# Cosine attention with a routed feed-forward: GpSimd's products held behind the transposes, gate rows spread over slots, square sums before the tail scores, and the last two batches' routed layers interleaved

## The chip, the cores and the metric

One core of a Trainium2 chip runs the whole program. The metric is device time in microseconds from the start of the program to its end. Engines: PE (matrix multiply; PEld is its weight load), DVE (vector), ACT (scalar), POOL (GpSimd), SP (issues DMAs). Each works through its own instructions in order and waits on semaphores for the others.

## The reference

```python
q_n = q / (norm(q) + 1e-6);  k_n = k / (norm(k) + 1e-6)      # (8, 12, 448, 64)
attn = softmax(q_n @ k_n.T / 0.1)
x = (attn @ v).transpose(0, 2, 1, 3).reshape(8, 448, 768)
scores = einsum('bsd,d->bs', x, w_gate)
for b in range(8):                                           # capacity 128
    top = the 128 rows of batch b with the largest scores
    xe = x[b, top]
    out[b, top] = x[b, top] + sigmoid(scores[b, top]) * (relu(xe @ w1) @ w2)   # w1 (768, 1024)
# all other rows of out are x
```

## The kernel before

**Attention.** The 96 heads are handled as 48 pairs, 6 pairs to a batch. Pair i has a *slot* i of the main loop (lines 591 to 641); the schedule is manual, so the order in which the code calls its helpers is the order of the instructions on every engine. The work of a slot is software-pipelined over four pairs:

- `square(p)` (L196, ACT) squares q and k of a pair about five slots ahead; `sum_pe` (L203, PE) and `sum_dve` (L209) add the squares up; `norm_a` (L217, L218, ACT) and `norm_b` (L223, L226, DVE) make the reciprocal norms for a group of up to three pairs.
- `scale(i+2)` (L236) multiplies q and k by the reciprocal norms into a buffer `qkn`, with two POOL instructions, and `values(i+2)` (L243, POOL) casts v. There are four `qkn` buffers (`NB`, L141).
- `transposes(i+1)` (L252 full tiles, L257 tails) turns them on PE into `qkT_ps`, and `qkT_copy` (L271, DVE) takes them to SBUF.
- `scores(i, c)` (L282; L287 for the tail c = 3) and `exps(i, c)` (L295; L298 for the tail) make the exponentials. They use a ring of two PSUM tiles `sc`, of two banks each; the sums of the squares go into the second bank of the tail's tile.
- `pv_tails(i-1)` and `pv(i-1)` (L309, L321) make the product with v, and `pv_evac` (L334, L335, DVE) divides by the row sums into `x_b`.

**Routed layer (MoE).** It runs batch by batch, woven into later slots. `at(slot, where, ...)` hangs a step on one of a slot's places (P, D1, A, D2, P2, C, B0, B), and the main loop calls the places in a fixed order. D1 and D2 stand before and after `pv_evac`, A between them, B at the slot's end. Its steps: `gate` (L357, DVE, one instruction for each of four row tiles j, two inputs in SBUF: `x_b` and `wg_b`), `rank_prep` (L366 to L375, POOL), `rank_rep` (L384, L387, PE), four `rank_count` (L396, DVE), four picks (L405, POOL) that make the one-hot `sel`, `select` (L416, PE, and L419 to L423, DVE), `gather` in two parts (L455, PE), `ffn1` in two halves (L469), `ffn2` in two halves (L482), and a scatter with add into the output (L488, an indirect DMA from POOL). All PSUM results of this layer share one bank (`bank`, L378). `store_x` (L344 to L349) writes x to the output from SP and a bf16 copy `xh` through POOL's queue, in two parts.

The last batch has its gates in three parts, over slots 46 to 48, and all its other steps stand after the loop (lines 644 to 656), each after the one before. Batch 6's `ffn1` second half and `ffn2` are in slot 48.

**Loads.** `load` (L98 to L114) issues eleven DMAs for a group of up to three pairs, from SP save for the keys of group 0, which ACT issues. Four raw buffers are used in turn. `load_wg` (L184) is the gate's weight, spread over 128 partitions, issued in slot 3; the weights w1 and w2 (L181) are loaded through POOL's queue in slots 3 and 6. `warm(n)` (L563) issues n idle matmuls of zeros.

Of the kernel before, what the change touches and what calls it, by code (L numbers as in the profile page):

```python
# [17 lines left out]
def kernel(  # L18
# [12 lines left out]
    nc = tc.nc  # L31
# [92 lines left out]
    load(1, 1, nc.sync)  # L124
    load(0, 2, nc.sync)
    load(1, 2, nc.sync)
    for which in range(3):
        load(2, which, nc.sync)

    iden_b = const.tile([P, P], BF16)  # L130
# [11 lines left out]
    kn_bufs = [const.tile([P, 2, NS, P], BF16, name=f"qkn{n}") for n in range(NB)]  # L142
# [18 lines left out]
    tie = const.tile([P, NS, S], BF16)  # L161
    iden_f = const.tile([P, P], FP32)
    ones_f = const.tile([P, P], FP32)
    nc.vector.memset(tie, 0.0)
    nc.vector.memset(ones_f, 1.0)
    wg_b = const.tile([P, D], FP32)
# [3 lines left out]
    def consts_a():  # L170
        nc.gpsimd.tensor_copy(iden_f, iden_b)

    def consts_tie(j):
        nc.gpsimd.affine_select(
            out=tie[:, j, :], in_=tie[:, j, :], compare_op=ALU.is_ge,
            fill=-(2.0 ** -126), base=-j * P, pattern=[[1, S]],
            channel_multiplier=-1)
# [35 lines left out]
    def norm_a(n):  # L213
        gn = NORMS[n][1]
        rs = prep.tile([P, 3, 2, NB7], FP32, name="rs", bufs=3)
        rs_tiles[n] = rs
        nc.scalar.activation(rs[:, :gn], ss_tiles[n][:, :gn], AF.Ln)  # L217
        nc.scalar.activation(rs[:, :gn], rs[:, :gn], AF.Exp, scale=0.5)  # L218

    def norm_b(n):  # L220
        gn = NORMS[n][1]
        r = rs_tiles[n][:, :gn].rearrange("p g a b -> p (g a b)")
        nc.vector.scalar_tensor_tensor(  # L223
            out=r, in0=r, scalar=1e-6, in1=zeros[:, :gn * 2 * NB7],
            op0=ALU.add, op1=ALU.add)
        nc.vector.reciprocal(r, r)  # L226

    def scale(p, engines=None):
        gi, g = place[p]
        n, m = nplace[p]  # L230
        qk = raw[gi % NRAW][0]
        rs = rs_tiles[n]
        kn = kn_bufs[p % NB]
        for eng, b0, nb, o in zip(engines or (nc.gpsimd, nc.gpsimd),
                                  (0, NS), (NS, NC), (0, Dh)):
            eng.tensor_mul(  # L236
                kn[:, :, :nb, o:o + Dh], qk[:, :, g, b0:b0 + nb],
                rs[:, m, :, b0:b0 + nb].rearrange("p a (b o) -> p a b o", o=1)
                .to_broadcast([P, 2, nb, Dh]))
# [7 lines left out]
    def transposes(p, part):  # L247
        kn = kn_bufs[p % NB]
# [26 lines left out]
    def scores(i, c):  # L275
        qkT = qkT_tiles[i]
        sc = ps_sc.tile([P, 2, 512], FP32, name="sc")
# [64 lines left out]
    def store_x(b):  # L342
        x_b = x_tiles[b]
        nc.sync.dma_start(out=out[b, :SM].rearrange("(m c) d -> m c d", c=NC),  # L344
                          in_=x_b[:, :NC])
        nc.sync.dma_start(out=out[b, SM:S], in_=x_b[:T, NC])
        xh = xp.tile([P, NS, D], BF16, name="xh")
        nc.gpsimd.dma_start(out=xh[:, :NC], in_=x_b[:, :NC])
        nc.gpsimd.dma_start(out=xh[:T, NC], in_=x_b[:T, NC])  # L349
        xh_tiles[b] = xh  # L350
# [27 lines left out]
    def bank():  # L378
        return ps_m.tile([P, 512], FP32, name="m_ps")
# [21 lines left out]
    def pick(b):  # L401
        sel = moe.tile([P, NS, CAP], BF16, name="sel")
        for j in range(NS):
            n = rows(j)
            nc.gpsimd.tensor_scalar(  # L405
                out=sel[:n, j], in0=iota_r[:n], scalar1=ranks[b % 2][:n, j:j + 1],
                scalar2=None, op0=ALU.is_equal)
        st[b]["sel"] = sel

    def select(b):  # L410
        sel, sg = st[b]["sel"], st[b]["sg"]
        pk = bank()
        for o, w, src in ((0, 2, tokc), (2, 3, sg)):
# [4 lines left out]
        pks = moe.tile([P, 2], FP32, name="pks")  # L418
        nc.vector.tensor_copy(pks, pk[:, 0:2])  # L419
        gr = moe.tile([P, 1], FP32, name="gr")  # L420
        nc.vector.tensor_reduce(gr, pk[:, 2:5], axis=AX.X, op=ALU.add)
        idx = moe.tile([P, 1], I32, name="idx")
        nc.vector.scalar_tensor_tensor(  # L423
            out=idx, in0=pks[:, 0:1], scalar=float(b * S), in1=pks[:, 1:2],
            op0=ALU.add, op1=ALU.add)
        st[b].update(idx=idx, gr=gr)

    def select_b(b):
        gr = st[b]["gr"]
        nc.scalar.activation(gr, gr, AF.Exp, scale=-1.0)  # L430
        nc.vector.scalar_tensor_tensor(out=gr, in0=gr, scalar=1.0, in1=zeros[:, :1],
                                       op0=ALU.add, op1=ALU.add)
        nc.vector.reciprocal(gr, gr)
# [12 lines left out]
    def gather(b, part, eng="D"):  # L446
# [3 lines left out]
        t0, t1 = ((0, 4), (4, KD))[part]  # L450
        ps = bank()
# [9 lines left out]
    def ffn1(b, part, eng="D"):  # L461
# [3 lines left out]
        ps = bank()  # L465
# [9 lines left out]
    def ffn2(b, n, eng="D"):  # L475
        hT = st[b]["hT"]
        if n == 0:
            st[b]["oe"] = moe.tile([P, D], FP32, name="oe")
        oe = st[b]["oe"]
        ps = bank()  # L480
        for t in range(KF):
# [3 lines left out]
        evac(eng, oe[:, n * ND:(n + 1) * ND], ps[:, :ND], AF.Copy,  # L485
             st[b]["gr"])
        if n == 1:
            nc.gpsimd.indirect_dma_start(  # L488
                out=out_flat[:, :],
                out_offset=bass.IndirectOffsetOnAxis(ap=st[b]["idx"][:CAP, 0:1],  # L490
                                                     axis=0),
                in_=oe[:CAP], in_offset=None, compute_op=ALU.add)
# [11 lines left out]
    for b in range(B - 2):  # L504
        s = HP * (b + 1)
        for j, (d, w) in enumerate(((1, "D1"), (1, "D2"), (2, "D1"), (2, "D2"))):
            at(s + d, w, gate, b, j)
        at(s + 3, "P", rank_prep, b)
        at(s + 3, "B", rank_rep, b)
        for j in range(NS):  # L510
            at(s + 4, "D1" if j < 2 else "D2", rank_count, b, j)
        at(s + 4, "P2", pick, b)
        at(s + 5, "A", select, b)
        at(s + 5, "C", select_b, b)
        at(s + 5, "B", gather, b, 0)
        at(s + 6, "A", gather, b, 1)
        at(s + 6, "B", ffn1, b, 0)
        late = b < B - 3
        at(s + 7, "B" if late else "A", ffn1, b, 1)
        at(s + 7 + late, "B", ffn2, b, 0)  # L520
        at(s + 8 + late, "A", ffn2, b, 1)
    b, bb = B - 2, B - 1
    s = HP * bb
    for j, (d, w) in enumerate(((0, "D2"), (1, "D1"), (1, "D1"), (1, "D2"))):
        at(s + d, w, gate, b, j)
    at(s + 2, "P", rank_prep, b)
    at(s + 2, "B0", rank_rep, b)
    for j in range(NS):
        at(s + 3, "D1" if j < 2 else "D2", rank_count, b, j)
    at(s + 3, "P2", pick, b)  # L530
    at(s + 4, "A", select, b)
    at(s + 4, "C", select_b, b)
    at(s + 4, "B", gather, b, 0)
    at(s + 5, "A", gather, b, 1)
    at(s + 5, "B", ffn1, b, 0)
    at(s + 6, "A", ffn1, b, 1, "A")
    at(s + 6, "A", ffn2, b, 0, "A")
    at(s + 6, "A", ffn2, b, 1, "A")
    ga = const.tile([P, NS], FP32)
    gb = const.tile([P, NS], FP32)  # L540
    for j in range(NS):
        at(N - 2, "D2", gate, bb, j, 0, 4 * P, None, ga)
        at(N - 1, "D2", gate, bb, j, 4 * P, 5 * P, ga, gb)
        at(N, "D2", gate, bb, j, 5 * P, D, gb)
    for b in range(B):
        at(HP * (b + 1), "D2", store_x, b)
    for j in range(NS):
        at(j, "P", consts_tie, j)
    at(0, "P", consts_a)
    at(3, "D1", load_wg)  # L550
    at(3, "P", load_w, w1_sb, moe_w1, kn_bufs[1][:, 1, 0, 0:1])
    at(6, "P", load_w, w2_sb, moe_w2, kn_bufs[0][:, 1, 0, 0:1])
# [12 lines left out]

    warm(30)
    for n in (0, 1):
        g0, gn = NORMS[n]
        sc = ps_sc.tile([P, 2, 512], FP32, name="sc")
        dst = [sc[:, 1, m * SW:(m + 1) * SW] for m in range(gn)]  # L570
        for m in range(gn):
            square(g0 + m)
        for m in range(gn):
            sum_pe(g0 + m, dst[m])
            sum_dve(g0 + m, dst[m])
        norm_a(n)
        norm_b(n)
        if n == 0:
            warm(50)
            scale(0, (nc.gpsimd, nc.vector))  # L580
            values(0)
# [3 lines left out]
        else:  # L585
            scale(1)
            values(1)
# [3 lines left out]
    for i in range(N + 1):  # L591
# [5 lines left out]
        run(i, "P")  # L597
# [6 lines left out]
        if live:  # L604
            exps(i, 0)
            exps(i, 1)
            for p in SQ.get(i, []):
                square(p)
# [5 lines left out]
        run(i, "P2")  # L614
        if i + 2 < N:
            scale(i + 2)
            values(i + 2)
# [4 lines left out]
        if live:  # L622
            scores(i, 3)
        if nxt:
            transposes(i + 1, 1)
            qkT_copy(i + 1)
        if live:
            exps(i, 2)
            sc = sc_tiles[i, 3]
            exps(i, 3)  # L630
            for m, p in enumerate(SQ.get(i, [])):
                dst = sc[:, 1, m * SW:(m + 1) * SW]
                sum_pe(p, dst)
                sum_dve(p, dst)
                n, g = nplace[p]
                if g == NORMS[n][1] - 1:
                    norm_a(n)
                    norm_b(n)
        run(i, "C")
        run(i, "B0")  # L640
        run(i, "B")
    assert not work, work

    rank_prep(bb)
    rank_rep(bb)
    for j in range(NS):
        rank_count(bb, j)
    pick(bb)
    select(bb)
    gather(bb, 0, "A")  # L650
    select_b(bb)
    gather(bb, 1, "D")
    ffn1(bb, 0, "A")
    ffn1(bb, 1, "D")
    ffn2(bb, 0, "A")
    ffn2(bb, 1, "D")
# [35 lines left out]
```

## Time and profile before

| | |
|---|---|
| median of 2 runs | 369.77 us (368.88 to 370.67) |
| the profiled execution | 371.18 us, of which 369.4 us are the span of the profile |
| PE busy | 281.0 us, 76% of the span |
| DVE busy | 206.6 us, 56% |
| ACT busy | 198.5 us, 54% |
| POOL busy | 178.8 us, 48% |
| mean granted PE clock | 0.892 |
| moved by DMA | 56.80 MB, 154 GB/s over the span |
| loop from slot 8 to the start of slot 48 | 69.96 to 326.58 us |
| from the last PV evacuation (329.2 us) to the end | 40.2 us |

In a line of the profile, `L203 PE MATMUL sc<-sq,iden_b` is the line of the kernel, the engine, the operation, and what is written from what. In the page's table of groups follow the shape, the number of instructions, their busy time and mean, and then how long the engine stood idle just before them and on whom it waited. A line of a timeline has the start, the duration and, in brackets, the idle time before. A busy share is a mean over the span; a stage's limit is read from its own timeline.

### The profile page before, as it was taken

To read this page: it belongs to the slowest core of one execution; us is meant where nothing else is said; L and a number is where in the kernel's file an instruction comes from. 1 tells how busy PE (TensorE), PEld (TensorE's weight loads), DVE (VectorE), ACT (ScalarE), POOL (GpSimd) and SP (SyncE) were. 2 spreads that over 40 slices of the span, in tenths; PEclk is the share of its full clock that TensorE was granted. 3 is DMA by queue.
4 is the path that set the end of the run, shared out by engine and by line. 5 is a ranking of instruction groups with operands and counts; after the bars stand their busy time and mean duration, and the time that the engine had idled before them with its cause. 6 is when DMAs were issued, how large, how long until landed. Compare 5 with 4: busy or idle time off the path is not lost.

```text
span 369.4 us, 8858 instructions
## 1 busy us (share of the span) xinstructions
PE 281.0 (76%) x3617; PEld 198.5 (54%) x3617; DVE 206.6 (56%) x476; ACT 198.5 (54%) x291; POOL 178.8 (48%) x267
## 2 busy tenths in 40 slices
PE   5729878587968887878798886979597878983570
PEld 5626555365754665556656565656465655662350
DVE  1213432657594669667865678566857786650300
ACT  2436787467655664767456674667557636320010
POOL 1347355347542947284825683566358528005201
PEclk9955898679998999999969999999999999577587
DMA  5799999999992859775963879596211533005503
GB/s 154 185 243 244 224 245 248 223 285 237 284 222 69 174 176 215 156 144 158 263 155 49 220 206 182 101 227 192 39 17 30 170 57 44 2 0 89 178 0 43
DMA packets 52744, 56.80 MB, mean 154 GB/s; under 512 B 9824, under 2 KB 48224, under 8 KB 51680
## 3 DMA queue, kind: packets, MB, share of 16 engines
q1 hardware_dynamic: 47616, 44.22, 45.0%
q0 software_dynamic: 4768, 11.80, 20.4%
q8 instruction: 28, 0.46, 0.5%
q10 hardware_dynamic: 320, 0.23, 0.2%
q14 instruction: 12, 0.10, 0.1%
HBM read 39.71 MB, written 14.16 MB: 146 GB/s over the span
## 4 chain that ended last, share of the span: by engine, by line
PE 34%; ACT 19%; DVE 14%; DMA 13%; issue 12%; SPq 3%; POOL 2%; POOLq 1%; DVEq 0%; ACTq 0%
ACT expS L295 12%; DMA qk_raw<-in_q_dram 7%; PE o_ps L321 7%; PE m_ps L482 6%; PE m_ps L455 5%; PE sc L282 5%; PE sc L203 4%; DVE junk L357 4%; ACT sq L196 3%; DMA wg_b<-in_moe_w_gate_dram 3%; DVE junk L396 3%; SPq L114 3%; ACT expS L298 3%; PE m_ps L469 3%; DVE qkT L271 2%
## 5 line engine op out<-in xcount | busy, mean ns | idle before, releaser
L295 ACT ACTIVATE expS<-sc 128x896 bf16<-128x896 f32 x144 | 126.7, 915 | 92.8 <-PE sc L282 92.0
L236 POOL TENSOR_TENSOR qkn<-qk_raw,rs 128x384 bf16<-128x384 f32 (+1 forms) x95 | 91.8, 1032 | 26.0 <-DVE rs L226 12.8
L321 PE MATMUL o_ps<-vo,expS 128*128 128x65 bf16 (+1 forms) x1152 | 64.5, 202 | 0.0
L203 PE MATMUL sc<-sq,iden_b 128*128 128x112 bf16 x384 | 29.5, 226 | 45.8 <-ACT expS L298 41.4
L282 PE MATMUL sc<-qkT 64*128 64x448 bf16 x288 | 50.5, 383 | 15.2 <-DVE qkT L271 13.2
L321 PEld LDWEIGHTS <-expS 128*128 128x128 bf16 (+1 forms) x1152 | 51.2, 104 | 10.0
L203 PEld LDWEIGHTS <-iden_b 128*128 128x128 bf16 x384 | 25.7, 105 | 51.8 <-issue 51.1
L357 DVE CUSTOM_DVE_ANT_0 junk<-x_b,wg_b 128x768 bf16<-128x768 f32 (+3 forms) x32 | 48.3, 1510 | 4.6 <-DMA wg_b<-in_moe_w_gate_dram 4.5
L196 ACT ACTIVATE sq<-qk_raw 128x896 bf16<-128x896 f32 x48 | 45.3, 951 | 6.7 <-DMA v_raw<-in_v_dram 4.3
L488 POOL DMA_INDIRECT out_dram<-oe,idx x8 | 13.6, 1701 | 64.8 <-DVE oe L442 44.5
L271 DVE COPY qkT<-qkT_ps 128x960 bf16<-128x960 bf16 x48 | 31.3, 652 | 14.8 <-PE qkT_ps L252 14.8
L334 DVE RECIPROCAL rden<-o_ps 128x8 f32<-128x8 f32 x48 | 9.9, 206 | 45.7 <-PE o_ps L321 45.6
L243 POOL CAST vo<-v_raw 128x448 bf16<-128x448 f32 x48 | 35.1, 731 | 0.5 <-DMA v_raw<-in_v_dram 0.5
L335 DVE TENSOR_TENSOR x_b<-o_ps,rden 128x512 f32<-128x512 f32 x48 | 33.2, 691 | 1.7
L209 DVE TENSOR_REDUCE ss<-sc 128x14 f32<-128x112 f32 x48 | 13.0, 272 | 31.8 <-PE sc L203 31.3
L366 POOL TENSOR_TENSOR diag<-iden_f,gate 128x512 f32<-128x512 f32 x8 | 8.9, 1117 | 41.4 <-DVE gate L357 41.4
L482 PE MATMUL m_ps<-w_sb,hT 128*128 128x384 bf16 x128 | 26.1, 351 | 3.5 <-DVE hT L438 1.5
L469 PE MATMUL m_ps<-xeT,w_sb 128*128 128x128 bf16 x384 | 26.5, 231 | 2.9 <-DVE hT L438 1.7
L282 PEld LDWEIGHTS <-qkT 64*128 64x128 bf16 x288 | 12.6, 95 | 29.7 <-DVE qkT L271 16.6
L405 POOL TENSOR_SCALAR sel<-iota_r,rank 128x128 bf16<-128x128 bf16 (+1 forms) x32 | 22.7, 854 | 10.8 <-DVE junk L396 10.1
L469 PEld LDWEIGHTS <-w_sb 128*128 128x128 bf16 x384 | 24.5, 104 | 3.4 <-issue 3.2
L298 ACT ACTIVATE expS<-sc 128x448 bf16<-128x448 f32 x48 | 26.2, 546 | 0.0
(75 smaller groups left out, 349.4 us busy)
## 6 DMA issues: line engine op xcount, KB each, us to landing
out_dram<-x_b SPq DMA_DIRECT2D x8, 1152.0 KB, 5.0
qk_raw<-in_q_dram SPq DMA_DIRECT2D x15, 576.0 KB, 7.1
qk_raw<-in_k_dram SPq DMA_DIRECT2D x30, 192.0 KB, 5.7
v_raw<-in_v_dram SPq DMA_DIRECT2D x30, 192.0 KB, 5.1
xh<-x_b POOLq DMA_DIRECT2D x8, 576.0 KB, 9.4
qk_raw<-in_k_dram SPq DMA_DIRECT2D x30, 144.0 KB, 5.4
v_raw<-in_v_dram SPq DMA_DIRECT2D x30, 144.0 KB, 4.3
w_sb<-in_moe_w_dram POOLq DMA_DIRECT2D x2, 1536.0 KB, 14.5
```

The costliest lines, as they stand in the source:

```text
L196: nc.scalar.activation(sq_tiles[p], raw[gi % NRAW][0][:, :, g].rearrange("p a b d -> p a (b d)") [:, :, :NB7 * Dh], AF.Square)
L203: nc.tensor.matmul(out=dst, lhsT=iden_b, rhs=sq[:, :, s * D8:(s + 1) * D8], start=(s == 0), stop=(s == Dh // D8 - 1))
L236: eng.tensor_mul(kn[:, :, :nb, o:o + Dh], qk[:, :, g, b0:b0 + nb], rs[:, m, :, b0:b0 + nb].rearrange("p a (b o) -> p a b o", o=1) .to_broa ...
L243: nc.gpsimd.tensor_copy(vo_bufs[p % NB][:, :, :Dh], raw[gi % NRAW][1][:, g, :NB7])
L271: nc.vector.tensor_copy(qkT_tiles[p], qkT_ps[:, :W])
L282: nc.tensor.matmul(out=sc[:, u, :S], lhsT=qkT[r, KO + c * P:KO + (c + 1) * P], rhs=qkT[r, :S], start=True, stop=True, tile_position=(u * D ...
L295: nc.scalar.activation(ex[:, 2 * c:2 * c + 2], sc[:, :, :S], AF.Exp, scale=inv_tau)
L298: nc.scalar.activation(ex[:, TAIL], sc[:, 0, :S], AF.Exp, scale=inv_tau)
L321: nc.tensor.matmul(out=o_ps[:n, u, j * E:(j + 1) * E], lhsT=ex[:, 2 * c + u, j * P:j * P + n], rhs=vo[:, u * NS + c], start=False, stop=(c ...
L357: nc.vector.tensor_tensor_reduce(out=junk[:n, d0:d1], in0=x_tiles[b][:n, j, d0:d1], in1=wg_b[:n, d0:d1], scale=1.0, scalar=0.0 if prev is ...
L469: nc.tensor.matmul(out=ps[:, f * CAP:(f + 1) * CAP], lhsT=w1_sb[:, t, fc * P:(fc + 1) * P], rhs=xeT[:, t], start=(t == 0), stop=(t == KD - 1))
L482: nc.tensor.matmul(out=ps[:, :ND], lhsT=hT[:, t], rhs=w2_sb[:, t, n * ND:(n + 1) * ND], start=(t == 0), stop=(t == KF - 1))
```

## The change

1. **One qkn buffer instead of four.** `scale(i+2)` and `values(i+2)` move from before the third scores to after the transposes, sums, tail scores and exponentials of the slot. As there is one buffer, the first product of `scale(i+2)` waits for the transposes of pair i+1.
2. **Slot order.** Tail and full transposes now stand together after the third scores, then `qkT_copy`; then the sums of squares, into a fresh `sc` tile, and the tail scores into the same tile behind them. The squares of pairs 3 and 4 move to the end of slot 0, and their sums to slot 1.
3. **Gate rows.** The four gate rows of a batch were two in slot s+1 and two in slot s+2 (s = 6(b+1)); now they are in slots s, s+1, s+2 and s+3, all in D2, and the later steps of the batch one slot later. Batches 4 to 6 have denser tables (two rows in one slot in slots 36, 42 and 43).
4. **Picks** move from POOL to DVE, after the counts in D2.
5. **Two-input DVE instructions** go: the epsilon of the norms and the 1 of the sigmoid are added by ACT (`AF.Identity` with a bias tile), and the index is made from a reduce and an add of a constant.
6. **POOL places.** `rank_prep`, `store_x`, weight loads and the scatter go to P2, which now stands after `scale` and `values`; xh is stored in one DMA.
7. **The end.** Batch 6's second half of `ffn1` and its `ffn2` go after the loop, between the last batch's steps; `bank(True)` gives them halves of the free `sc` tiles. The last gate part is one product and one reduce. The last batch's store stands ahead of the scatter of batch 6, and its two `ffn2` halves need not wait for both halves of `ffn1`.
8. **The start.** The keys of groups 1 and 2 are issued by ACT, group 2's q and k come ahead of the values; `warm(50)` becomes `warm(24)`, with eight idle matmuls twice in slots 0 to 2.

```diff
-    load(1, 1, nc.sync)
+    load(1, 1, nc.scalar)
+    load(2, 0, nc.sync)
+    load(2, 1, nc.scalar)
     load(0, 2, nc.sync)
     load(1, 2, nc.sync)
-    for which in range(3):
-        load(2, which, nc.sync)
+    load(2, 2, nc.sync)
...
-    kn_bufs = [const.tile([P, 2, NS, P], BF16, name=f"qkn{n}") for n in range(NB)]
+    kn = const.tile([P, 2, NS, P], BF16, name="qkn")
...
         nc.scalar.activation(rs[:, :gn], rs[:, :gn], AF.Exp, scale=0.5)
+        nc.scalar.activation(rs[:, :gn], rs[:, :gn], AF.Identity, bias=epsb[:, 0:1])
...
-        nc.vector.scalar_tensor_tensor(
-            out=r, in0=r, scalar=1e-6, in1=zeros[:, :gn * 2 * NB7],
-            op0=ALU.add, op1=ALU.add)
         nc.vector.reciprocal(r, r)
...
-        nc.gpsimd.dma_start(out=xh[:, :NC], in_=x_b[:, :NC])
-        nc.gpsimd.dma_start(out=xh[:T, NC], in_=x_b[:T, NC])
+        nc.gpsimd.dma_start(out=xh, in_=x_b)
...
-            nc.gpsimd.tensor_scalar(
+        nc.vector.tensor_scalar(
...
+    def bank(big=False):
+        if not big:
+            return ps_m.tile([P, 512], FP32, name="m_ps")
+        if not wide:
+            t = ps_sc.tile([P, 2, 512], FP32, name="sc")
+            wide.extend((t[:, 1], t[:, 0]))
+        return wide.pop()
...
+    late = dict(gate=(0, 1, 2, 3), prep=3, rep=4, rank=5, select=6, gather=7,
+                ffn=((7, "B"), (8, "B"), (9, "B"), (10, "A")), scatter=10)
...
         run(i, "D2")
-        run(i, "P2")
-        if i + 2 < N:
-            scale(i + 2)
-            values(i + 2)
+        if i < 3:
+            warm(8)
         if live:
             scores(i, 2)
         if nxt:
             transposes(i + 1, 0)
-        if live:
-            scores(i, 3)
-        if nxt:
             transposes(i + 1, 1)
             qkT_copy(i + 1)
         if live:
+            sc = ps_sc.tile([P, 2, 512], FP32, name="sc")
+            sq = (SQ[0] if i == 1 else []) + (SQ.get(i, []) if i else [])
+            sums(sq, sc)
+            scores(i, 3, sc)
             exps(i, 2)
-            sc = sc_tiles[i, 3]
             exps(i, 3)
...
         run(i, "C")
-        run(i, "B0")
+        if i + 2 < N:
+            scale(i + 2)
+            values(i + 2)
+        run(i, "P2")
+        if i < 3:
+            warm(8)
         run(i, "B")
...
+    store_x(bb)
+    xg = moe.tile([P, NS, P], FP32, name="xg", bufs=1)
+    nc.vector.tensor_mul(
+        xg, x_tiles[bb][:, :, 5 * P:D],
+        wg_b[:, 5 * P:D].rearrange("p (o d) -> p o d", o=1).to_broadcast([P, NS, P]))
+    gc = moe.tile([P, NS], FP32, name="gc", bufs=1)
+    nc.vector.tensor_reduce(gc, xg, axis=AX.X, op=ALU.add)
+    g = gates[bb % 2]
+    nc.vector.tensor_add(g, gc, gb)
+    b = B - 2
+    ffn1(b, 1, "A", True)
     rank_prep(bb)
+    ffn2(b, 0, "A", True)
     rank_rep(bb)
+    ffn2(b, 1, "A", True)
     for j in range(NS):
         rank_count(bb, j)
-    pick(bb)
-    select(bb)
-    gather(bb, 0, "A")
-    select_b(bb)
-    gather(bb, 1, "D")
-    ffn1(bb, 0, "A")
-    ffn1(bb, 1, "D")
-    ffn2(bb, 0, "A")
-    ffn2(bb, 1, "D")
+        pick(bb, j)
+    scatter(b)
+    gather(bb, 0, "A", True, 3)
+    gather(bb, 1, "D", True, 3)
+    select(bb)
+    select_b(bb)
+    ffn1(bb, 0, "A", True)
+    ffn1(bb, 1, "D", True)
+    ps = [bank(True), bank(True)]
+    for h in range(2):
+        for n in range(2):
+            ffn2_mm(bb, n, ps[n], h * 4, h * 4 + 4)
+    ffn2_evac(bb, 0, ps[0], "A")
+    ffn2_evac(bb, 1, ps[1], "D")
+    scatter(bb)
```

## The prediction

> **What bounds the kernel now.** I read the page's groups first, then the timelines of PE, DVE and POOL, then the chain. The two groups that carry the prediction (busy, mean ns, idle before and its releaser):
>
> ```profile
> L203 PE MATMUL sc<-sq,iden_b 128*128 128x112 bf16 x384 | 29.5, 226 | 45.8 <-ACT expS L298 41.4
> L357 DVE CUSTOM_DVE_ANT_0 junk<-x_b,wg_b 128x768 bf16<-128x768 f32 (+3 forms) x32 | 48.3, 1510 | 4.6 <-DMA wg_b<-in_moe_w_gate_dram 4.5
> ```
>
> PE waits 41.4 us for the tail exponential before it may sum squares into the same PSUM tile. A gate row averages 1510 ns though most take 950. PE's timeline of one slot without A or B work:
>
> ```profile
> 199.68 0.55 PE L282 MATMUL sc<-qkT 64*128 64x448 bf16 x4
> 200.07 0.40 PE L309 MATMUL o_ps<-vo,expS 64*128 64x65 bf16 x8
> 200.41 1.27 PE L321 MATMUL o_ps<-vo,expS 128*128 128x65 bf16 x24
> 201.61 0.36 PE L282 MATMUL sc<-qkT 64*128 64x448 bf16 x2
> 201.90 0.25 PE L257 MATMUL qkT_ps<-iden_b,qkn 64*64 64x64 bf16 x4
> 202.08 0.36 PE L287 MATMUL sc<-qkT 128*128 128x448 bf16 x1
> 202.28 0.50 PE L252 MATMUL qkT_ps<-iden_b,qkn 128*128 128x128 bf16 x6
> 203.94 0.55 PE L203 MATMUL sc<-sq,iden_b 128*128 128x112 bf16 x8 [1.16 <-ACT expS L298]
> ```
>
> The next slot starts at 204.59: of 4.91 us, 1.16 are that wait. DVE and POOL, where a batch's first gate row is due:
>
> ```profile
> 177.93 4.64 DVE L357 CUSTOM_DVE_ANT_0 junk<-x_b,wg_b 128x768 bf16<-128x768 f32 x1
> 183.35 0.95 DVE L357 CUSTOM_DVE_ANT_0 junk<-x_b,wg_b 128x768 bf16<-128x768 f32 x1
> ```
> ```profile
> 177.63 1.84 POOL L236 TENSOR_TENSOR qkn<-qk_raw,rs 128x512 bf16<-128x512 f32 x2
> 179.42 0.55 POOL L243 CAST vo<-v_raw 128x448 bf16<-128x448 f32 x1
> 179.93 1.82 POOL L236 TENSOR_TENSOR qkn<-qk_raw,rs 128x512 bf16<-128x512 f32 x2
> 181.71 1.27 POOL L243 CAST vo<-v_raw 128x448 bf16<-128x448 f32 x1
> ```
>
> The row ends just after the last product of POOL's burst; the cast behind it is stretched from 0.55 to 1.27. qkT's copy queues behind the row, so PE idles 1.56 us. First rows start at 100.40 and 255.92, four batches apart: 38.9 us a batch. The chain, start and end of the kernel (start, us, what):
>
> ```profile
> 53.76 12.20 DMA wg_b<-in_moe_w_gate_dram
> ...
> 314.59 20.06 issue
> ...
> 334.90 0.75 POOL out_dram L488
> ...
> 337.79 1.08 POOL diag L366
> ```
>
> POOL holds batch 6's scatter first, so the last xh store and diag, whose gates were ready at 330.93, wait behind it.
>
> [...]
>
> **The loop, part by part.** Times count from a slot's first scores. PE's shares, start to start, warm: scores 0.39, tail PV 0.34, PV 1.20 (ends at 1.93), third scores 0.29, transposes 0.18 and 0.33 (last lands at 2.90), tail scores 0.20, sums 0.40. MoE: select 0.43, gathers 1.57 and 0.71, ffn1 1.44 a half, ffn2 1.41 a half, rep 1.02.
>
> *Sums ahead of tail scores.* The wait on the tail exponential (0.64 or 1.16 a slot) goes; sums now wait for the square. ACT starts at 0.41, two exponentials take 1.61, the square 0.9: 2.95. PE reaches sums at 2.73 without A work: 0.25 lost instead. Sums end at 3.4, tail scores at 3.6; tail exponential ends at 4.3, before the next scores want its tile where B work follows.
>
> *One gate row per slot; products after transposes.* PV's evacuation ends at 2.80 (x_b starts 0.35 after PV's end; the next DVE row 0.61 later). Bare slot: row at 2.80, transposes land at 2.90, POOL reacts 0.07 later (gate end 188.77 to diag 188.84), at 2.97. So the row is first by 0.1-0.2 us, takes 0.95; POOL waits; qkT is copied by 4.4, under B work. With select or gather1 in A, DVE's evacuation of 0.26 or 0.42 precedes the row, transposes come 0.43 or 0.71 later: margin 0.3 to 0.5. POOL then needs 0.95+2.4 us; the next transposes come over 4 us later, so the single qkn buffer costs nothing.
>
> Slots of one batch, by offset: 0 (select, gather0) 5.5, with 0.2 of it ACT's later start behind a norm; 1 (gather1, ffn1) 5.5; 2 and 3 (ffn1; ffn2) 5.0 each; 4 (ffn2, rep) 5.8. Slot 5 is DVE's: two counts early, evacuation to 2.8, two counts to 4.3, four picks, copy 0.65. [...]the trace's nearest, a 128x2 copy, is 0.15. Free, the slot is 5.4; with picks behind POOL's burst (2.97 plus 2.4, stretched by the counts' reads) 6.6. I take 6.6, since POOL starts first. Sum 33.4; 0.08 a slot between instructions 0.5; one half-clock spell of PE after slot 5's idle 3 us, between 0 and 3, taken 1.0: 34.9, say 35.0 a batch, 5.83 a slot.
>
> Slots 8 to 47 took 69.96 to 326.58 = 256.6. Now 40 x 5.83 = 233.3: **-23.3**.
>
> *Two rows in one slot* (slots 36, 42, 43): the second row meets POOL already waiting, loses 1.83, plus its own 0.95; between 0 and 2.5 each, taken 1.7: **+5**.
>
> *Small edits.* Epsilon by ACT is one more instruction per norm group: 0.24 like its neighbours[...]. ACT is busy 198.5/48 = 4.1 of a 5.8 us slot, and the reciprocal behind it is due a slot later: booked 0. The two-input SBUF add that goes sat once 3.03 behind POOL, and idx sat 1.47 in most batches; both fell inside slots already counted. POOL loses the picks (22.7/8 = 2.8 a batch) and half of the xh issue (0.6). Moved past the products to P2, xh store, weight loads and the batch's rank preparation start about 3 later in their slot; gather reads xh a batch later, rep reads diag a slot later (ready 2.4 before it), so nothing. On SP the store of x passes no load. On POOL the queue behind a held product is cast, xh, rank preparation and scatter, and the next transposes wait for it with 4 to spare; on DVE the copy of qkT waits behind picks and rows, and PE behind it: that is counted above. Behind sums held by a square stand tail scores and B work: also counted.
>
> **The start.** ACT issues eight more DMAs before its first square: 8 x 0.66 (four took 2.64) after the table load at 4.67, so 10 instead of 6.60: +3.4. Against that, group 2's keys arrive early, and the hole 19.5 to 27.6 before slot 1 closes. Slot 6 would start some 8 us earlier, near 46-48. But its gate row needs wg_b, still issued behind fifteen pairs of loads; the DMA engines are full from 18 us on. Before: issued 53.76, landed 65.96. With perhaps 3 us of faster ramp: 62.5. Row 0.95, copy 0.65: slot 7 at 64.2; a cold slot of 6.5: slot 8 at 70.7 against 69.96: **+0.7**, bounds -6 and +5. The early gain is swallowed by this DMA.
>
> **The tail.** Before: slot 48 begins at 326.58, end 369.4: 42.8. Now: PV and evacuation 2.5 (T). Gate by product and reduce 1.6, diag 1.04: T+2.7; rep by T+3.8, own 0.2, four counts and picks of 1.05: T+8.2. The xh store, issued at once beside the output store, needs a median of 9.5 (7.0 to 11.1): gather at T+10.2, this bounds. Two half gathers, cold 2.0 each, evacuation 0.5, select 0.7 beneath it: T+14.9. ffn1 2.3 and 1.44, ffn2 2.92 with no wait between halves, evacuation 0.62: T+22.2. Scatter from evacuation's end to the end: 8.3 as before (361.06 to 369.4). T+30.5, so 33.0: **-9.8**.
>
> Sum: 369.4 - 23.3 + 5 + 0.7 - 9.8 = 342.0 of span. The median 369.77 is 0.4 above this span (that execution took 371.18): 342.4.
>
> **Rivals.**
> *Bare-slot races lost* (17%): the rows of offsets 2 and 3 come 0.1 late. Row waits to 4.8, ends 5.7, copy 6.3 against 5.0: 1.3 twice a batch, 6.67 batches: +17, 360. For it: the margin is a tenth; against: evacuation and transposes hang on the same PV end, so the order repeats.
> *GpSimd always first, slower* (13%): [...]offsets 0 and 1 lose 1.25 and 1.4 as well: 5.3 a batch, +35, 378. It decides once a product starts before its slot's row, that is, with DVE's evacuation 0.3-0.5 later against the transposes than the trace shows. For it: 4.64 us rows exist today. Against: those meet a POOL running late behind xh, here cleared by about 1.1 of the next slot.
> *[...]clock full* (10%): picks unblocked (-1.2), no cold spell (-1.0) a batch, two-row slots free: -20, 323.
> *The wait only changes name*: sums now wait for squares by 1.2 rather than 0.25 in every slot; +38 would undo everything. The square's place at 2.95 speaks against; I leave 5% for this and any other unforeseen wait.
>
> The forecast has 55%: 330 to 353 by its own bounds. Eight in ten: 323 to 367. Two per cent is about what a measurement here tells from no change: 362.4 to 377.2. Faster 0.76 (forecast, better case, most of the first rival), same 0.11, slower 0.13.
>
> **What would show it.** L203's idle on ACT near zero and slots near 5.8; gate rows at 0.95 in offsets 0 to 3 with POOL's first product stretched instead; picks of over 1 us in offset 5; a long DVE wait on wg_b around 50-62; the last gather released by xh, with diag right after the gate. Gate rows of 2.8 and more in every batch would break the forecast; so would a wait for squares of a microsecond at the sums.

## The result, and the profile after

The changed kernel took 404.94 us (median of 2 runs, 403.85 to 406.02) against 369.77 before: ratio 1.095 [1.078, 1.112]. The forecast was 342.4, range 323 to 367. The profiled execution's span is 404.2, at a granted clock of 0.76 (before 0.89).

The groups of the page after (busy, mean ns, idle before and its releaser):

```profile
L286 PE MATMUL sc<-qkT 128*128 128x448 bf16 x48 | 20.7, 431 | 41.4 <-DVE ss L211 41.4
L205 PE MATMUL sc<-sq,iden_b 128*128 128x112 bf16 x384 | 33.8, 245 | 13.9 <-ACT sq L198 11.3
L355 DVE CUSTOM_DVE_ANT_0 junk<-x_b,wg_b 128x768 bf16<-128x768 f32 (+3 forms) x32 | 30.8, 963 | 0.2
```

Two things went as meant. The sums no longer wait for the tail exponential (of their 11.3 us on squares, 9.4 is one wait at the start), and gate rows average 963 ns instead of 1510. But PE still waits 41.4 us, now at the tail scores (L286), for VectorE's reduce of the sums (L211). The chain that ended last shows what this leads to (start, us, what):

```profile
59.28 0.96 DVE junk L355
60.24 0.01 DVE gate L355
60.25 0.57 DVE qkT L269
60.82 0.19 DVE ss L211
61.01 0.04 issue
61.05 0.36 PE sc L286
61.42 0.02 issue
61.44 0.55 ACT expS L297
61.99 0.04 issue
62.03 0.36 PE sc L281 x2
62.40 0.24 PE o_ps L308 x8
62.64 1.37 PE o_ps L320 x24
64.01 0.02 issue
64.03 0.22 DVE rden L333
64.25 0.02 issue
64.27 0.69 DVE x_b L334
64.96 0.86 DVE junk L355
```

Read it as a ring: gate row, qkT copy and reduce on VectorE, then tail scores, tail exponential, the next slot's scores and PV, the evacuation, and the next gate row. Each step of the ring starts as the one before it ends: 59.28 to 64.96 is one round, 5.68 us. VectorE's share of the chain is 25%, before 14%.

PE in a slot with a gate row (its first scores start at 204.00), and in a rank slot (222.88); then VectorE in the same two slots:

```profile
207.02 0.55 PE L205 MATMUL sc<-sq,iden_b 128*128 128x112 bf16 x8
208.65 0.35 PE L286 MATMUL sc<-qkT 128*128 128x448 bf16 x1 [1.07 <-DVE ss L211]
...
225.96 0.55 PE L205 MATMUL sc<-sq,iden_b 128*128 128x112 bf16 x8 [0.17 <-ACT sq L198]
229.45 0.35 PE L286 MATMUL sc<-qkT 128*128 128x448 bf16 x1 [2.93 <-DVE ss L211]
```
```profile
206.89 0.95 DVE L355 CUSTOM_DVE_ANT_0 junk<-x_b,wg_b 128x768 bf16<-128x768 f32 x1
207.76 0.65 DVE L269 COPY qkT<-qkT_ps 128x960 bf16<-128x960 bf16 x1
208.33 0.27 DVE L211 TENSOR_REDUCE ss<-sc 128x14 f32<-128x112 f32 x1
...
226.48 0.68 DVE L401 SCALAR_TENSOR_TENSOR junk<-m_ps,own,tie 64x448 bf16<-64x448 f32 x1
227.09 0.07 DVE L401 DVE_READ_ACCUMULATOR junk<-m_ps,own,tie 64x1 f32 x1
227.09 1.55 DVE L410 TENSOR_SCALAR sel<-iota_r,rank 128x128 bf16<-128x128 bf16 x4
228.57 0.64 DVE L269 COPY qkT<-qkT_ps 128x960 bf16<-128x960 bf16 x1
229.14 0.25 DVE L211 TENSOR_REDUCE ss<-sc 128x14 f32<-128x112 f32 x1
```

In the rank slot the sums are done at 226.5, but their reduce stands behind a count, four picks and the copy until 229.4; the tail scores go the moment it ends. What follows the 2.93 us is seen in the windows of one batch (us, then busy time and count per engine, PE's granted clock, DMA share, GB/s):

```profile
190.00:204.00 14.00, 13.27 (x120) 9.52 (x118) 5.67 (x13) 5.56 (x9) 5.22 (x7) 0.52 0.99 260
204.00:230.00 26.00, 20.01 (x276) 13.81 (x275) 15.62 (x38) 16.09 (x23) 14.14 (x19) 1.00 0.52 119
230.00:248.00 18.00, 16.93 (x166) 12.15 (x164) 7.31 (x19) 9.39 (x16) 5.22 (x7) 0.53 0.76 203
248.00:275.00 27.00, 20.68 (x288) 14.19 (x287) 15.62 (x38) 16.73 (x25) 14.15 (x19) 1.00 0.54 115
```

From 204 to 230 PE has full clock (1.00) although it is idle a quarter of the time (20.01 us busy of 26.00), until the rank slot's gap; then it has half clock (0.53). This repeats in every batch, with 17 to 24 us at half clock each time. Counted in windows of 1 us between 55 and 313 us, PE is at half clock for 123 us, before for 24.

### The profile page after: what moved, and what is told of

It reads as the page before. It is cut to its first block, busy times and chain, and to the rows that moved or that the text cites. A ratio compares the mean times of both kernels' runs of the same rounds, so it can differ in the third digit from the quotient of the medians.

```text
span 404.2 us, 8840 instructions
## 1 busy us (share of the span) xinstructions
PE 321.2 (79%) x3639; PEld 223.8 (55%) x3639; DVE 186.4 (46%) x481; ACT 209.4 (52%) x317; POOL 159.3 (39%) x227
## 4 chain that ended last, share of the span: by engine, by line
PE 57%; DVE 25%; DMA 8%; ACT 3%; issue 2%; SPq 2%; POOL 1%; POOLq 0%; ACTq 0%
PE o_ps L320 16%; PE sc L281 7%; PE m_ps L456 7%; PE m_ps L470 6%; DVE junk L355 5%; DVE qkT L269 5%; PE sc L286 5%; DVE x_b L334 4%; PE m_ps L479 4%; PE o_ps L308 3%; DVE sel L410 3%; DMA qk_raw<-in_q_dram 3%; DMA qk_raw<-in_k_dram 2%; PE qkT_ps L250 2%; DVE junk L401 2%; DMA xh<-x_b 2%
## 5 line engine op out<-in xcount | busy, mean ns | idle before, releaser
L320 PE MATMUL o_ps<-vo,expS 128*128 128x65 bf16 (+1 forms) x1152 | 72.3, 215 | 0.0
L281 PE MATMUL sc<-qkT 64*128 64x448 bf16 x288 | 58.3, 433 | 9.3 <-DVE qkT L269 5.2
L286 PE MATMUL sc<-qkT 128*128 128x448 bf16 x48 | 20.7, 431 | 41.4 <-DVE ss L211 41.4
L205 PE MATMUL sc<-sq,iden_b 128*128 128x112 bf16 x384 | 33.8, 245 | 13.9 <-ACT sq L198 11.3
L470 PEld LDWEIGHTS <-w_sb 128*128 128x128 bf16 x384 | 31.2, 121 | 10.7 <-issue 10.0
L355 DVE CUSTOM_DVE_ANT_0 junk<-x_b,wg_b 128x768 bf16<-128x768 f32 (+3 forms) x32 | 30.8, 963 | 0.2
L456 PEld LDWEIGHTS <-xh 128*128 128x128 bf16 x192 | 17.2, 120 | 24.5 <-issue 15.7
L250 PE MATMUL qkT_ps<-iden_b,qkn 128*128 128x128 bf16 x288 | 30.1, 254 | 0.9 <-POOL qkn L235 0.9
L456 PE MATMUL m_ps<-sel,xh 128*128 128x128 bf16 (+1 forms) x168 | 28.5, 301 | 0.0
L308 PEld LDWEIGHTS <-expS 64*128 64x128 bf16 (+1 forms) x384 | 19.8, 110 | 13.1 <-issue 3.8
L242 POOL CAST vo<-v_raw 128x448 bf16<-128x448 f32 x48 | 26.6, 555 | 0.0
```

The lines of the kernel that those rows point to most:

```text
L205: nc.tensor.matmul(out=dst, lhsT=iden_b, rhs=sq[:, :, s * D8:(s + 1) * D8], start=(s == 0), stop=(s == Dh // D8 - 1))
L281: nc.tensor.matmul(out=sc[:, u, :S], lhsT=qkT[r, KO + c * P:KO + (c + 1) * P], rhs=qkT[r, :S], start=True, stop=True, tile_position=(u * D ...
L286: nc.tensor.matmul(out=sc[:, 0, :S], lhsT=qkT[:, KT:W], rhs=qkT[:, :S], start=True, stop=True)
L320: nc.tensor.matmul(out=o_ps[:n, u, j * E:(j + 1) * E], lhsT=ex[:, 2 * c + u, j * P:j * P + n], rhs=vo[:, u * NS + c], start=False, stop=(c ...
L355: nc.vector.tensor_tensor_reduce(out=junk[:n, d0:d1], in0=x_tiles[b][:n, j, d0:d1], in1=wg_b[:n, d0:d1], scale=1.0, scalar=0.0 if prev is ...
L456: nc.tensor.matmul(out=ps[:, (t - t0) * CAP:(t - t0 + 1) * CAP], lhsT=xh[:n, j, t * P:(t + 1) * P], rhs=sel[:n, j], start=(j == 0), stop=( ...
```

## Experiments

Each first number is the median of four executions in us. The ratio, with its 95% interval, is always to the kernel before, run on the same chip (medians 369 to 372). "Half clock" is the count just described, in the one execution that was profiled.

**1 to 4: the changed kernel with one thing undone.** The first two ask whether the wait for the reduce is the cause, the third takes VectorE's work out of its way, the fourth fills the gap with idle matmuls (on zeros, into unused columns, so nothing computed changes).

```diff
 # e1: back behind the tail exponential, from slot 2
-            sums(sq, sc)
             scores(i, 3, sc)
             exps(i, 2)
             exps(i, 3)
+            sums(sq, sc)
 # e2: the output tile's unused columns instead of the tail scores' tile
-            sums(sq, sc)
+            sums(sq, o_ps, NS * E)
 # e3: rows, later counts, picks behind copy and reduce
-        run(i, "D2")
...
             sums(sq, sc)
             scores(i, 3, sc)
+            run(i, "D2")
 # e4: rank slots only
             sums(sq, sc)
+            for _ in range(44):
+                nc.tensor.matmul(out=o_ps[:, 0, 384:512], lhsT=zeros_b, rhs=zeros_b,
+                                 start=True, stop=True)
             scores(i, 3, sc)
```

> The changed kernel with one part undone: the sums of squares stand behind the tail exponential again (from slot 2 on). Theory (the tail scores wait for DVE's reduce of the sums, because both lie in one PSUM tile, and PE's long wait in rank slots then halves its clock): the wait of tail scores on the reduce (41.4 us) goes, sums wait again for the tail exponential (about 0.7 us a slot), slots of 6.1 to 6.4, some 37 us a batch in place of 44.3: 355 us. Rival (the DVE queue is what costs: rows, picks and the copy of qkT ahead of the next scores, whatever waits for it on PE): the wait turns up at the next scores instead, 390 to 404 us.

> The changed kernel with the sums in columns of the PV result's tile that nothing else uses, so that the tail scores wait neither for the reduce nor the sums for the tail exponential; the order is unchanged. Theory: slots without a rank lose their 1.07 us, 35 to 37 us a batch if PE keeps its clock, 345 to 355 us. In rank slots PE still idles about 2.7 us for the copy of qkT behind the picks; if that alone halves the clock for 20 us a batch, 375 us. Rival (DVE's queue): the wait moves to the next scores, 390 to 404 us.

> The changed kernel with gate rows, later counts and picks (place D2) behind the copy of qkT and the reduce in DVE's order. Theory: the tail scores then wait for the copy and the reduce alone, 0.5 us; the rank slot shrinks from 6.85 to about 4.5 and PE keeps its clock; gate rows now meet POOL's burst and take up to 2.8 us, which nobody waits for: 33 to 35 us a batch, 327 to 340 us. Rival (rows behind POOL's burst hold the next evacuation, and the clock falls all the same): 385 us or more, with rows of 2.8 us released late and PV's tile waiting.

> The changed kernel with 44 idle matmuls of zeros (about 2.5 us at full clock) between sums and tail scores in the rank slots alone; no result changes. Theory: they fill the 2.9 us in which PE waits for the reduce, so its clock stays full in the two slots after; 6.8 us a batch come back, the ordinary wait of 1.07 us stays: 359 us. Rival (the clock follows from the lower load in all slots and not from this gap): mean clock stays near 0.76, 400 us or more, up to 420 us if the idle matmuls lengthen the slot.

- e1: 399.78 us, 1.085 [1.076, 1.093]; half clock 130 (in an execution of 405.05). My theory's number missed by 45 us, and the rival's 390 to 404 holds. With the sums put back, the rank slot waits for the tail exponential and then for the copy behind the picks (PE's timeline of e1):

```profile
228.32 0.56 PE L205 MATMUL sc<-sq,iden_b 128*128 128x112 bf16 x8 [1.22 <-ACT expS L297]
230.39 0.93 PE L281 MATMUL sc<-qkT 64*128 64x448 bf16 x4 [1.52 <-DVE qkT L269]
```

- e2: 349.85, 0.951 [0.942, 0.960]; half clock 79. The order is the same, but the sums no longer share the tail scores' tile: 55.1 us less than the changed kernel, within the 345 to 355 expected, though the clock wasn't kept as that assumed. In the output's tile, which they share now, the longest of their waits in the loop is 0.7 us. What waits now is the scores for the qkT copy (20.1 us).
- e3: 326.53, 0.888 [0.881, 0.895], half a us below the 327 to 340 expected; half clock 10. The tile is still shared, but the reduce has nothing of this work ahead of it except the copy. The wait falls from 41.4 to (waits of e3: us, times, longest)

```profile
PE sc L286 <- DVE ss L211: 18.6, 42, 0.5
```

- e4: 385.14 (373.2 to 387.5), no ratio, because its executions differ with the clock (0.88 to 0.94); half clock 65 (in the one of 387.5). This lies between the two expectations: with the rank slots' gap filled, half clock falls to about half but doesn't end, and the tail scores still wait 33.4 us for the reduce.

**5, 6 and 9: the kernel before with one part of the change.** e5 puts the sums ahead of the tail scores, in their tile; e6 has one qkn buffer and the products held behind the transposes; e9 puts all but the last batch's picks on VectorE.

```diff
 # e5
+                sum_pe(p, dst)
+                sum_dve(p, dst)
+            scores(i, 3, sc)
             exps(i, 2)
             exps(i, 3)
 # e6: behind the slot's "C" work; kn_bufs[0] for every pair
-        if i + 2 < N:
-            scale(i + 2)
-            values(i + 2)
         if live:
             scores(i, 2)
...
         run(i, "C")
+        if i + 2 < N:
+            scale(i + 2)
+            values(i + 2)
 # e9
-        at(s + 4, "P2", pick, b)
+        at(s + 4, "D2", pick, b, nc.vector)
```

> The kernel before with one edit: from slot to slot the eight sums go into the tail scores' tile ahead of the tail scores, behind the qkT copy, as in the changed kernel; nothing held, rows two to a slot, picks still on GpSimd. Theory (the shared tile makes the tail scores wait for VectorE's reduce, and VectorE's queue ahead of it decides): the wait for the reduce appears at the scores' line with 25 to 50 us in all, the wait for the tail exponential goes, and the time is 370 to 395. Rival (the order of the sums alone is a gain, and it is the picks and the hold that spoil it in the changed kernel): 340 to 355.

> The kernel before with one edit: one qkn buffer, and GpSimd's two products and value copy emitted behind the slot's norms, so that they are held behind the pair's transposes; sums behind the tail exponential, rows two to a slot, picks on GpSimd. Theory: the rows of 4.64 us are gone (rows 0.95 to 2.3), worth 5 to 10 us of the 369, so 358 to 366 if the clock stays as before; picks on GpSimd stand in the queue as before. Rival (the hold makes the transposes late by GpSimd's 4 us and costs clock): over 375, with waits of the transposes on qkn over 20 us.

> The kernel before with one edit: the four picks of every batch's rank slot except the last batch's go from GpSimd to VectorE, behind the later two counts and ahead of the qkT copy. Theory (picks ahead of the qkT copy make the rank slot late by some 1.5 us and with that bring half clock, which is why the changed kernel stays at 400 with its sums back behind the tail exponential): half clock between 55 and 313 us rises from 24 us to over 60, 375 to 395. Rival (picks are cheap on VectorE unless the tail scores wait behind them): 364 to 372.

- e5: 408.69, 1.100 [1.092, 1.109]; half clock 105. Slower than expected: the row of 4.62 us, which the hold would have removed, now stands ahead of the reduce (VectorE, then PE, of e5):

```profile
153.93 4.62 DVE L358 CUSTOM_DVE_ANT_0 junk<-x_b,wg_b 128x768 bf16<-128x768 f32 x1
...
160.77 0.26 DVE L209 TENSOR_REDUCE ss<-sc 128x14 f32<-128x112 f32 x1
```
```profile
161.08 0.53 PE L288 MATMUL sc<-qkT 128*128 128x448 bf16 x1 [4.29 <-DVE ss L209]
```

- e6: 356.16, 0.958 [0.952, 0.965], 2 us better than expected; half clock 32. The hold, with the one buffer, is a gain by itself, and the long rows are gone (group of e6):

```profile
L357 DVE CUSTOM_DVE_ANT_0 junk<-x_b,wg_b 128x768 bf16<-128x768 f32 (+3 forms) x32 | 30.6, 956 | 0.1
```

- e9: 401.82, 1.081 [1.071, 1.090], above the 395 expected; half clock 79. The picks alone cost a lot: they stand ahead of the copy, take 0.65 us each, and PE stands still behind them (VectorE, then PE, of e9):

```profile
171.55 2.58 DVE L405 TENSOR_SCALAR sel<-iota_r,rank 128x128 bf16<-128x128 bf16 x4
174.05 0.64 DVE L271 COPY qkT<-qkT_ps 128x960 bf16<-128x960 bf16 x1
```
```profile
174.75 0.66 PE L282 MATMUL sc<-qkT 64*128 64x448 bf16 x4 [2.59 <-DVE qkT L271]
```

**7, 8, 10, 11: which of VectorE's work, and which order.** e7 and e8 split e3. e10 is e1 with the rows, later counts and picks moved behind the copy, e11 is e2 with them behind copy and reduce, as in e3.

```diff
 # e7: "D3" runs behind sums and tail scores
-            at(s + m["rank"], "D1" if j < 2 else "D2", rank_count, b, j)
+            at(s + m["rank"], "D1" if j < 2 else "D3", rank_count, b, j)
-            at(s + m["rank"], "D2", pick, b, j)
+            at(s + m["rank"], "D3", pick, b, j)
 # e8
-            at(s + m["gate"][j], "D2", gate, b, j)
+            at(s + m["gate"][j], "D3", gate, b, j)
```

> The changed kernel with only the later two counts and the four picks emitted behind the reduce on VectorE; the gate rows stay where they were, ahead of the qkT copy. Theory (the rank slot's counts and picks ahead of the reduce open the 2.9 us wait that ends in half clock): the clock stays full through the loop, the rank slot's wait is under 1 us, the wait of 1.0 in the row slots stays, 335 to 350. Rival (any wait of 1 us in a slot is enough to lose the clock): spells of half clock once a batch remain, 365 to 395.

> The changed kernel with only the gate rows emitted behind the reduce; counts and picks stay ahead of it. Theory: the rank slot's 2.9 us wait remains, with it the half clock once a batch, 375 to 400. Rival (rows cost as much as picks): 340 to 365.

> The changed kernel with both suspects put back: sums behind the tail exponential again from slot 2, and gate rows, later counts and picks behind the qkT copy on VectorE. Theory (what the slots can't stand is VectorE's rows, counts and picks ahead of what PE waits for; the order of the sums matters only through that): waits for the tail exponential of about 35 us in all return, the clock stays full, 328 to 345, a little slower than the 326.5 with the sums ahead. Rival (a wait behind the tail exponential, 1 us, loses the clock as well): 365 to 400.

> The changed kernel with the sums in the unused columns of the output's PSUM tile, and gate rows, later counts and picks behind the reduce: the wait for the reduce (18.6 us in all with the shared tile) can't occur. Theory (that wait is on the path of PE at full clock): 308 to 322. Rival (the slot is then bound by something else, ScalarE's exponentials or the qkT copy, and the wait only moves): 323 to 330.

- e7: 360.74 (352.7 to 368.9), no ratio, because the executions differ by too much; half clock 38 (in one of 359.5), of which 27 is one spell at 62 to 89. From 89 to 249 the clock is full, as the theory says, although rows still make PE wait (over the whole run the tail scores wait 33.3 us for the reduce, at most 2.7 at once). But two spells remain, and even the fastest execution is above its 350.
- e8: 383.61, 1.036 [1.028, 1.044]; half clock 89. Counts and picks left in front keep a rank-slot wait of up to 3.0 us, as expected.
- e10: 384.35, 1.030 [1.018, 1.042], so slower, but not clearly by 2%; half clock 119. The number missed, but the edit isn't what the expectation took it for. The sums, and with them the reduce, now come last in the slot, so rows, counts and picks stand behind the copy and still ahead of the reduce, for which the next scores wait. In the slot after which the clock falls, PE stands still twice within 3.1 us (PE, then VectorE, of e10):

```profile
179.82 0.55 PE L205 MATMUL sc<-sq,iden_b 128*128 128x112 bf16 x8 [1.22 <-ACT expS L297]
181.66 0.56 PE L281 MATMUL sc<-qkT 64*128 64x448 bf16 x2 [1.00 <-DVE ss L211]
```
```profile
178.45 0.66 DVE L269 COPY qkT<-qkT_ps 128x960 bf16<-128x960 bf16 x1
...
180.35 1.08 DVE L410 TENSOR_SCALAR sel<-iota_r,rank 128x128 bf16<-128x128 bf16 x4
181.36 0.26 DVE L211 TENSOR_REDUCE ss<-sc 128x14 f32<-128x112 f32 x1
```

So e10 doesn't refute the theory. The sums behind the tail exponential with all of this work behind the reduce too were not run.

- e11: 304.41, 0.818 [0.811, 0.825]; half clock 12. The fastest of all, and below the 308 expected. No wait for the reduce at the tail scores is left; PE is busy 86% of the span.

**12: the gap by itself.** The e11 version, with the first count of the batch repeated four times ahead of the copy in the loop's rank slots.

```diff
+            at(s + m["rank"], "X", rank_count, b, 0)   # once for each j
...
         run(i, "A")
+        run(i, "X")
```

> The version with own columns for the sums and rows, later counts and picks behind the reduce (304.4 us), with one thing added: in each rank slot of the loop (seven) VectorE repeats the first count four times behind the output's evacuation and ahead of the qkT copy (4 x 0.75 = 3.0 us), so that PE stands still for about 2.5 to 3 us once a batch; the repeats rewrite the same ranks. It measures the price of one such gap by itself. Theory (a gap of nearly 3 us drops the granted clock to half for 7 to 20 us after it): half clock between 55 and 313 us rises from 12 us to over 60, and the time is over 304 + 7 x 3 = 325: 340 to 375. Rival (the gap costs its own length only, and half clock in the changed kernel has another cause): 318 to 326.

343.64 us, 0.925 [0.920, 0.930]; half clock 71. The waits of e12, and one of them:

```profile
PE sc L281 <- DVE qkT L269: 18.7, 7, 3.3
```
```profile
190.71 0.55 PE L281 MATMUL sc<-qkT 64*128 64x448 bf16 x4 [2.55 <-DVE qkT L269]
```

Seven gaps of 18.7 / 7 = 2.7 us cost 343.64 - 304.41 = 39.2 us, 5.6 each: the gap itself and as much again, with half clock for 6.8 to 13.7 us at each of the first six and 17.1 at the last. The rival's 318 to 326 is excluded.

The changed kernel's versions side by side (us):

| sums | rows, later counts, picks ahead of the copy | behind copy and reduce |
|---|---|---|
| ahead, tail scores' tile | 404.9 (the change) | 326.5 (e3) |
| ahead, own columns | 349.9 (e2) | 304.4 (e11) |
| behind the tail exponential | 399.8 (e1) | not run; behind the copy, ahead of the reduce: 384.4 (e10) |

## Why the prediction was wrong

**The step that failed** is "Sums end at 3.4, tail scores at 3.6". It lets the tail scores start when the sums end. They write bank 0 of the tile whose bank 1 the reduce reads, and the wait goes by the tile: 41.4 us of it at L286 for L211, and none when the sums have other columns (e2). So they start when the reduce ends, and the prediction had the rest of the sum: row at 2.80, "qkT is copied by 4.4", and a reduce of 0.25 makes 4.65. The slot that starts at 204.00 has its tail scores at 208.65: 4.65. In the rank slot they come at 6.57. The profile before had the clue: there the sums waited 41.4 us for an exponential that reads the other bank of the same tile. I took that for something which the new order removes, and didn't ask who reads the tile next. The rival "the wait only changes name" had 5% and named the squares; those are no wait (0.17). The runs show the cause. With the sums in the output's tile and nothing else changed, 55.1 us go (e2): the 349.85 that remain are within the forecast's own 330 to 353, with more half clock than it had. With the tile still shared and VectorE's rows, counts and picks behind the reduce, 78.4 us go (e3). In the kernel before, this order of sums and tail scores alone costs 10% (e5).

**The second wrong term** is the clock, "taken 1.0" a batch, which was my estimate. One batch took 44.3 us against 35.0:

| slots | predicted | measured |
|---|---|---|
| offsets 0 and 1 (half clock) | 11.0 | 9.08 + 9.53 = 18.6 |
| offsets 2, 3, 4 | 15.8 | 6.28 + 6.21 + 6.39 = 18.9 |
| offset 5 (rank) | 6.6 | 6.85 |
| gaps, spell, rounding | 1.6 | in the above |

7.6 of the difference are the two slots at half clock, and 3.1 are offsets 2 to 4 at full clock, mostly their waits (1.07, 1.06 and 0.54). Slots 8 to 48 took 303.8 us against 233.3 + 5, and that is all of the error. The clock term depends on the first: e12 shows that a gap of 2.7 us costs 5.6, and of the 123 us at half clock 79 remain when the tile is no longer shared (e2), but 10 when VectorE's other work goes behind the reduce (e3). The rank slot's length was nearly right, 6.85 for 6.6, by luck, as it had the wrong owner. That the picks wait for GpSimd's products was my estimate; in the slot shown four picks start at 227.09, while the products run to 227.77, and take 0.39 each (0.25 in the tail), and PE stands still in one piece behind them (2.93).

**What held.** Rows were mostly not held up by GpSimd's products: 963 ns on average, the longest 1769. Where a row starts ahead of the two products (206.89 against 207.07) these take 2.47 us, against 1.83 with no row beside them (at 200.54). The hold alone is worth 4% (e6). The start: slot 8 at 67.10, 2.9 earlier than before, where +0.7 with -6 to +5 was given; wg_b was issued at 44.6, not near 50.7, and no row waits for it. The tail: 370.92 to 404.2 is 33.3 against 33.0, bound as foreseen by the xh store (the chain after):

```profile
373.81 9.03 DMA xh<-x_b
```

Of the two-row slots' +5 only slot 36 can be told apart: it took 10.73 us where that offset took 9.08 to 9.27 in the four batches before, near the 1.7 taken for one. With the wait at 0.5 us at most, e3's batch is 34.6 us against the 35.0 of the forecast, though by another split: its rank slot is 4.28.

## What to carry to other kernels

When work is moved into a PSUM tile ahead of its old user, ask who reads that tile next and what stands ahead of that reader on its engine: a wait that goes by whole tiles (here 41.4 us in all) ties that engine's queue into every step. Emit what PE waits for (copy, reduce) ahead of what nobody waits for yet (rows, counts, picks). Price a gap of PE of nearly 3 us at more than its length (here 5.6 us for 2.7, in e12), and look at the granted clock by stage.

## What the runs showed of the hardware

- In the changed kernel, six of the seven spells of half clock that begin between 55 and 317 us start during a wait of PE of 2.92 to 2.99 us for the reduce, or at most 1.3 us after it; the first starts at 63.40, and in the 8 us before it no single wait is over 0.82. In the two rank slots of e12 whose timeline was read, the gaps are 2.55 and 2.56 us, and half clock starts 1.6 and 0.9 us after them. In e10 it starts at 181.4, in the second of two waits (1.22 and 1.00) with work between them. Single waits of 0.64 or 1.16 us, as in four slots of e6 between 150 and 174, mostly kept full clock (e6: 32 us of 258 at half).
- The spells of the changed kernel's loop last 17.1 to 23.9 us, those of e12's 6.8 to 17.1. PE's busy time alone doesn't tell the clock: in the changed kernel PE is busy 20.01 of 26.00 us (77%) from 204 to 230, at full clock (1.00), but 16.34 of 17.07 us (96%) from 230.67 to 247.74, at half (0.50), and all of the 3.41 us after that at full again. What ends a spell was not shown.
- In e11 gate rows start while GpSimd's products run (a row at 176.88, products from 176.20 to 178.75), and the four of the batch from 175 to 194 take 1.08 to 1.21 us, not the 4.6 of the kernel before. Why rows take so much longer beside one burst than beside the other is open.
